# Four 32-column tiles in place of one 128-column matmul, in the MLP of an attention + MLP kernel

## The chip, the cores and the metric

The kernel runs on one core of a Trainium2 chip. Times are device microseconds (us) of one execution, medians over several executions. The record marks all timed runs used here as fast. Runs made once, for a look with a profile, have the state "unknown" and are compared only for effects of several microseconds, or by what their trace shows.

## The reference, cut to what matters

```python
scores = q @ k^T / 8 + decay, causal          # 64 (batch, head) pairs, 576 x 576, head 64
attn   = softmax(scores) @ v                  # gathered to x: 4608 tokens x 512
h      = x @ w_in                             # 512 -> 2048
out    = gelu_tanh(h) @ w_out                 # 2048 -> 512, float32
```

## The kernel before: the parts that matter

TensorE uses its array in three shapes, which the profile prints as rows*columns. Scores use 32 rows and 128 columns (32*128; each head's data lies on 32 partitions). Attention products use 128 rows and 32 columns (128*32). The MLP's matmuls used the full array (128*128), except where L368 stood beside attention products: there it was already cut into four tiles of 32 columns.

```python
    def mlp_in(c, prs):                       # hidden layer, 512 tokens at a time
        ...
                        nc.tensor.matmul(
                            ph[:, j, :],
                            w_in_sb[:, dt, 128 * ft:128 * ft + 128],
                            xT[:, dt, CH * c:CH * (c + 1)],
                            start=(dt == 0), stop=(dt == N_DT - 1))       # L330
    def mlp_in_half(half, g):                 # the first 512 tokens, 256 at a time
        ...
                    nc.tensor.matmul(
                        ph[:, j // 2, QA * (j % 2):QA * (j % 2) + QA],
                        w_in_sb[:, dt, 128 * ft:128 * ft + 128],
                        xT[:, dt, n0:n0 + QA], ...)                       # L347
    def mlp_out(c):
        ...
                    cols = 32 if by_columns else 128
                    for c0 in range(0, 128, cols):
                        nc.tensor.matmul(pso[c0:c0 + cols, m0:m1],
                                         gT[c % 2][:, ft, 128 * n + c0:128 * n + c0 + cols],
                                         w_out_sb[:, ft, m0:m1], ...)     # L368
```

L347 stands early in the kernel, while w_in, w_out, q, k and v are still being loaded. The keep-busy matmuls of zeros (L199) and the prefix sums stay full in both kernels.

The softmax here doesn't subtract the row's maximum and nothing guards it: scores larger than these inputs give would overflow.

Of the kernel before, what the change touches and what calls it, by code (L numbers as in the profile page):

```python
# [16 lines left out]
def kernel(  # L17
# [10 lines left out]
    nc = tc.nc  # L28
# [10 lines left out]
    N_DT = D_MODEL // 128  # L39
# [6 lines left out]
    CH = 512  # L46
# [12 lines left out]
    QA = 256  # L59
# [33 lines left out]
    def many(n, shape, dtype, name):  # L93
        return [singles.tile(shape, dtype, name=f"{name}{i}") for i in range(n)]
# [13 lines left out]
    xT = singles.tile([128, N_DT, B * S], BF16, name="xT")  # L108
    gT = many(2, [128, N_FT, CH], BF16, "gT")
    w_in_sb = singles.tile([128, N_DT, D_FF], BF16, name="w_in_sb")  # L110
# [91 lines left out]
    def scores(i, r, groups=((0, 1, 2, 3),)):  # L202

        qq, p = qT[i % 2], pt[i % 2]
        if i < 2:
            off, n = split_rounds[r]
            todo = [(key, col - off, q0, nq) for (key, col, q0, nq) in split_pieces[r]]
        else:
            off, n = rounds[r]
            todo = []  # L210
            for (key, col, q0, nq) in pieces:
                a, z = max(col, off), min(col + nq, off + n)
                if a < z:
                    todo.append((key, a - off, q0 + a - col, z - a))
        for heads in groups:
            tiles = {g: psS.tile([128, 2, 512], FP32, name="ps_s", tag="s") for g in sorted({h // 2 for h in heads})}
            for c in range(2):
                for j, (key, c0, q0, nq) in enumerate(todo):
                    for h in heads:
                        nc.tensor.matmul(  # L220
                            tiles[h // 2][:, h % 2, c0:c0 + nq],
                            key_columns(i, key, h, c),
                            qq[32 * h:32 * h + 32, q0:q0 + nq, c],
                            start=(c == 0 and j == 0), stop=(c == 1),
                            skip_group_check=True,
                        )
            for g, t in tiles.items():
                nc.scalar.activation(p[:, 2 * g:2 * g + 2, off:off + n], t[:, :, 0:n], AF.Exp, scale=scale)  # L228
# [93 lines left out]
    def mlp_in(c, prs):  # L322

        tiles = [psS.tile([128, 2, 512], FP32, name="ps_h", tag="s") for _ in prs]
        for pr, ph in zip(prs, tiles):
            for dts in (range(N_DT - 1), range(N_DT - 1, N_DT)):
                for j in range(2):
                    ft = 2 * pr + j
                    for dt in dts:
                        nc.tensor.matmul(  # L330
                            ph[:, j, :],
                            w_in_sb[:, dt, 128 * ft:128 * ft + 128],
                            xT[:, dt, CH * c:CH * (c + 1)],
                            start=(dt == 0), stop=(dt == N_DT - 1),
                        )
        for pr, ph in zip(prs, tiles):
            nc.scalar.activation(gT[c % 2][:, 2 * pr:2 * pr + 2, :], ph, AF.Gelu_apprx_tanh)  # L337

    def mlp_in_half(half, g):

        ph = psS.tile([128, 2, 512], FP32, name="ps_h", tag="s")
        n0 = QA * half
        for dts in (range(N_DT - 1), range(N_DT - 1, N_DT)):
            for j in range(4):
                ft = 4 * g + j
                for dt in dts:
                    nc.tensor.matmul(  # L347
                        ph[:, j // 2, QA * (j % 2):QA * (j % 2) + QA],
                        w_in_sb[:, dt, 128 * ft:128 * ft + 128],
                        xT[:, dt, n0:n0 + QA],  # L350
                        start=(dt == 0 and j % 2 == 0), stop=(dt == N_DT - 1),
                        skip_group_check=True,
                    )
        nc.scalar.activation(gT[0][:, 4 * g:4 * g + 4, n0:n0 + QA],
                             ph.rearrange("p a (b n) -> p (a b) n", n=QA), AF.Gelu_apprx_tanh)

    def mlp_out(c):

        for n in range(CH // 128):
            r0 = CH * c + 128 * n  # L360
            last = c == NCH - 1 and n == CH // 128 - 1
            st = ostage_pool.tile([128, D_MODEL], FP32, name="o_st", tag="o")
            for (m0, m1) in ((0, 384), (384, 512)) if last else ((0, D_MODEL),):
                pso = psM.tile([128, D_MODEL], FP32, name="pso", tag="m")
                for ft in range(N_FT):
                    cols = 32 if by_columns else 128
                    for c0 in range(0, 128, cols):
                        nc.tensor.matmul(pso[c0:c0 + cols, m0:m1],  # L368
                                         gT[c % 2][:, ft, 128 * n + c0:128 * n + c0 + cols],
                                         w_out_sb[:, ft, m0:m1],  # L370
                                         start=(ft == 0), stop=(ft == N_FT - 1), skip_group_check=True)
                    if ft == N_FT - 1:
                        nc.vector.tensor_copy(st[:, m0:m1], pso[:, m0:m1])  # L373
                        eng = nc.scalar if m0 else nc.sync
                        eng.dma_start(out=out[r0:r0 + 128, m0:m1], in_=st[:, m0:m1])
                    yield
# [56 lines left out]
                cum_ps[:rows, t0 * BH:t1 * BH].rearrange("p (t i h) -> p t i h", i=NQ, h=4),  # L433
                AF.Exp, scale=-1.0, bias=shift[:rows, :])

    by_columns = []

    def pull(it, n):
        for _ in range(n):
            if next(it, False) is False:  # L440
                return
# [1 line left out]
    fills = {}  # L443
    dmas = {}

    def out_part(c, n, tiled=0):
        by_columns[:] = [True] * tiled
        pull(fills.setdefault(c, mlp_out(c)), n)

    def cast_w(copy):  # L450
# [3 lines left out]
    def load_values(b, half):  # L454
# [29 lines left out]
        "WI": load_w_in,  # L484
        "WO": load_w_out,
        "I": lambda c, pr: mlp_in(c, (pr,)),
        "J": mlp_in_half,
        "F": out_part,
        "f": lambda c, n: out_part(c, n, 1),
        "B": keep_busy,  # L490
        "X": load_exp,
    }
# [12 lines left out]
    def beside(i, r, c, todo):  # L505

        if i is not None:
            scores(i, r)
        for n, x in enumerate(todo):
            if isinstance(x, int):  # L510
                out_part(c, x, 1)
            else:
                x()
            if n == 0 and i is not None:
                after_scores(i, r)

    def after_scores(i, r):
        mask(i, r)
        if r == 1:
            make_vw(i, nc.gpsimd)  # L520
        if r == 2:
            copy_low(i)

    def pair(i, j, c):

        D, V = (lambda q: lambda: denominators(q)), (lambda q, x, spare=False: lambda: attn_out(q, x, spare))
        beside(i, 0, c, [D(j), 12])
        beside(i, 1, c, [V(j, 0), 10])
        beside(i, 2, c, [V(j, 1), 9])
        if i + 1 < NQ:  # L530
            beside(i + 1, 0, c, [D(i), 10])
            beside(i + 1, 1, c, [V(i, 0), 5, V(i, 1), 4])
            scores(i + 1, 2)
            after_scores(i + 1, 2)
        else:
            beside(None, 0, c, [D(i), 10, V(i, 0), V(i, 1, True), 10])
# [11 lines left out]
    with tc.manual_schedule():  # L548
        setup()
        run(FRONT)  # L550
        for c in range(2, NCH):
            out_part(c - 1, CH)
            for pr in range(2):
                mlp_in(c, (pr,))
            if c + 1 < B:
                prepare(2 * c + 3, 2 * c + 4)
            if c + 2 < B:
                load_v(c + 2)
            for pr in range(2, NP):
                mlp_in(c, (pr,))  # L560
            if c + 1 < B:
                load_exp()
                out_part(c, 6)
                pair(2 * c + 3, 2 * c + 2, c)
        out_part(NCH - 1, CH)
# [30 lines left out]
```

## Time and profile before

| | before |
|---|---|
| median of 6 runs | 341.67 us (341.55 to 342.11) |
| span of the profiled run | 339.9 us |
| TensorE busy | 329.8 us (97%) |
| TensorE matmuls, and as many weight loads | 4241 |

The lines that show the bound and the pitches are in the prediction. Two more views follow. First the DMA queue that carries instructions: packets, megabytes, and the time that they took as a share of 16 DMA engines. A packet has 16 KB (0.54 MB in 33).

```profile
q8 instruction: 33, 0.54, 0.7%
```

Then the early stretch of L347 in TensorE's timeline (start, duration, group; "x96" counts instructions):

```profile
27.79 1.92 PE L347 MATMUL ps_h<-xT,w_in_sb 128*128 128x256 bf16 x16
29.64 1.22 PE L274 MATMUL po_m<-pt,vw 128*32 128x320 bf16 x40
30.79 10.65 PE L347 MATMUL ps_h<-xT,w_in_sb 128*128 128x256 bf16 x96
41.28 1.46 PE L368 MATMUL pso<-w_out_sb,gT 128*128 128x512 bf16 x6
```

96 matmuls start within 41.28 - 30.79 = 10.49 us, 109 ns each, with nothing between them. ("128x256" means 256 moving columns: the columns of the operand that streams through the array.)

### The profile page before, as it was taken

The numbers are of one execution on the slowest core, as the hardware profiler recorded it, in microseconds if no ns is written. First come the engines' busy times: TensorE is split into PE (matmuls) and PEld (weight loads), VectorE is DVE, ScalarE is ACT, GpSimd is POOL, SyncE is SP. The second block draws the span as 40 slices with busy tenths as digits, with TensorE's granted clock in tenths as the row PEclk, the third lists the DMA queues.
The fourth block names the chain that finished last, engine by engine and source line by source line (L and its number), as shares of the span: only waits on it lengthen the run. The fifth ranks groups of instructions, "written<-read, shape, count | busy, mean of one in ns | idle before, by whom it ended". The sixth has DMA issues, their size and how long they took to land.

```text
span 339.9 us, 9423 instructions
## 1 busy us (share of the span) xinstructions
PE 329.8 (97%) x4241; PEld 162.0 (48%) x4241; DVE 132.3 (39%) x206; ACT 191.8 (56%) x201; POOL 110.1 (32%) x155
## 2 busy tenths in 40 slices
PE   3999999999999999999999999999999999999996
PEld 1458844544454445444444444444544454444443
DVE  4686059830465435703462244413430450021011
ACT  4784686677547665667566665674576624502510
POOL 8987551600506233601551145106410410000000
PEclk9999999999999999999999999999999999999999
DMA  7999999570316970591129210910100010011012
GB/s 127 207 216 214 196 230 194 102 172 2 95 36 101 227 156 33 131 205 39 35 77 207 59 67 35 212 30 35 63 31 2 33 63 34 2 62 62 0 40 85
DMA packets 40201, 33.26 MB, mean 98 GB/s; under 512 B 27473, under 2 KB 29777, under 8 KB 40161
## 3 DMA queue, kind: packets, MB, share of 16 engines
q0 software_dynamic: 8848, 16.58, 27.4%
q1 hardware_dynamic: 31168, 16.01, 17.0%
q8 instruction: 33, 0.54, 0.7%
q10 hardware_dynamic: 144, 0.07, 0.1%
q14 instruction: 8, 0.06, 0.0%
HBM read 36.85 MB, written 9.44 MB: 136 GB/s over the span
## 4 chain that ended last, share of the span: by engine, by line
PE 90%; DMA 2%; POOL 2%; ACT 2%; DVE 1%; issue 1%; POOLq 0%; DVEq 0%; ACTq 0%
PE pso L368 36%; PE ps_h L330 33%; PE po L288 8%; PE ps_s L220 8%; PE ps_h L347 4%; DMA v_nat<-in_v_dram 2%; ACT pt L228 2%; PE po_m L274 1%; POOL vw L178 1%; POOL v_nat L132 0%; PE ps_o L288 0%; DVE pt L263 0%; DVE vw L178 0%; POOL pt L234 0%; POOL q_c L155 0%
## 5 line engine op out<-in xcount | busy, mean ns | idle before, releaser
L368 PE MATMUL pso<-w_out_sb,gT 128*32 128x512 bf16 (+3 forms) x1492 | 134.5, 377 | 0.0
L228 ACT ACTIVATE pt<-ps_s 128x1024 bf16<-128x1024 f32 (+2 forms) x100 | 93.7, 988 | 53.6 <-PE ps_s L220 46.0
L330 PE MATMUL ps_h<-xT,w_in_sb 128*128 128x512 bf16 x512 | 111.9, 379 | 0.0
L337 ACT ACTIVATE gT<-ps_h 128x1024 bf16<-128x1024 f32 x64 | 65.5, 1024 | 64.1 <-PE ps_h L330 64.1
L234 POOL TENSOR_SCALAR_AFFINE_SELECT pt<-pt 128x512 bf16<-128x512 bf16 (+3 forms) x65 | 38.2, 597 | 140.6 <-ACT pt L228 139.7
L368 PEld LDWEIGHTS <-gT 128*32 128x32 bf16 (+1 forms) x1492 | 56.3, 97 | 56.8 <-issue 3.5
L330 PEld LDWEIGHTS <-w_in_sb 128*128 128x128 bf16 x512 | 50.0, 98 | 60.4 <-issue 0.4
L373 DVE COPY o_st<-pso 128x512 f32<-128x512 f32 (+2 forms) x37 | 24.9, 673 | 71.8 <-PE pso L368 71.5
L307 DVE STREAM_TRANSPOSE den<-po 128x576 f32<-128x576 f32 x14 | 11.0, 784 | 65.7 <-PE po L288 65.7
L220 PE MATMUL ps_s<-qT,kT 32*128 32x64 bf16 (+5 forms) x896 | 36.2, 264 | 0.2 <-ACT pt L228 0.2
L319 DVE TENSOR_TENSOR xT<-po,rb 128x576 bf16<-128x576 f32 x26 | 19.7, 757 | 31.6 <-PE po L288 31.5
L178 POOL TENSOR_TENSOR vw<-v_nat,wT 128x1280 bf16<-128x1280 f32 (+1 forms) x13 | 30.0, 2308 | 0.1
L220 PEld LDWEIGHTS <-kT 32*128 32x128 bf16 x896 | 16.4, 93 | 23.7 <-issue 18.8
L161 DVE STREAM_TRANSPOSE kT<-k_c 128x576 f32<-128x576 f32 x16 | 20.0, 1248 | 16.9 <-DMA k_c<-in_k_dram 16.8
L288 PE MATMUL po<-pt,vw 128*32 128x64 bf16 (+4 forms) x624 | 22.4, 278 | 0.0
L161 DVE STREAM_TRANSPOSE qT<-q_c 128x576 f32<-128x576 f32 x16 | 19.9, 1244 | 1.2 <-PE ps_s L220 0.7
L288 PEld LDWEIGHTS <-vw 128*32 128x32 bf16 x672 | 14.2, 97 | 11.8 <-issue 3.7
L132 POOL DMA_DIRECT2D v_nat<-in_v_dram x20 | 15.3, 776 | 3.4 <-DMA w_out_sb<-in_moe_w_out_dram 3.4
L347 PE MATMUL ps_h<-xT,w_in_sb 128*128 128x256 bf16 x128 | 14.5, 273 | 0.0
L347 PEld LDWEIGHTS <-w_in_sb 128*128 128x128 bf16 x128 | 12.3, 98 | 1.7
L311 DVE STREAM_TRANSPOSE rb<-rec 128x576 f32<-128x576 f32 (+2 forms) x18 | 12.8, 711 | 0.6
L155 POOL DMA_DIRECT2D k_c<-in_k_dram x16 | 9.1, 568 | 11.3 <-DVE kT L161 5.7
(61 smaller groups left out, 124.9 us busy)
## 6 DMA issues: line engine op xcount, KB each, us to landing
out_dram<-o_st SPq DMA_DIRECT2D x35, 256.0 KB, 2.1
k_c<-in_k_dram POOLq DMA_DIRECT2D x16, 288.0 KB, 6.8
q_c<-in_q_dram POOLq DMA_DIRECT2D x16, 288.0 KB, 7.4
v_nat<-in_v_dram SPq DMA_DIRECT2D x16, 256.0 KB, 8.3
w_in_sb<-in_moe_w_in_dram POOLq DMA_DIRECT2D x4, 512.0 KB, 9.5
w_out_sb<-in_moe_w_out_dram POOLq DMA_DIRECT2D x4, 512.0 KB, 7.2
v_nat<-in_v_dram SPq DMA_DIRECT2D x16, 128.0 KB, 3.3
v_nat<-in_v_dram POOLq DMA_DIRECT2D x13, 128.0 KB, 7.9
```

Of the source, the lines that this page charges most:

```text
L161: nc.vector.transpose(out=dst.rearrange("p s c -> p (s c)").bitcast(FP32) .rearrange("p (t a) -> p a t", a=S // 32), in_=src.rearrange("p ...
L178: eng.tensor_mul(vw[i % 2][:, t0:t1], vb[:, t0:t1, h0:h0 + 4, :], wT[:, i, t0:t1, :].unsqueeze(3).to_broadcast([128, t1 - t0, 4, D]))
L220: nc.tensor.matmul(tiles[h // 2][:, h % 2, c0:c0 + nq], key_columns(i, key, h, c), qq[32 * h:32 * h + 32, q0:q0 + nq, c], start=(c == 0 an ...
L228: nc.scalar.activation(p[:, 2 * g:2 * g + 2, off:off + n], t[:, :, 0:n], AF.Exp, scale=scale)
L234: nc.gpsimd.affine_select(out=x, in_=x, compare_op=ALU.is_ge, fill=0.0, base=0, pattern=pattern, channel_multiplier=-1)
L288: nc.tensor.matmul(po[r0:r0 + w.shape[-1], 448 + q0:448 + q0 + nq], w, p[:, h, col:col + nq], start=(key in (0, "low")), stop=(key in ("lo ...
L319: nc.vector.tensor_mul(xT[:, 2 * u + x, S * b + s0:S * b + s1], po, rbs[i, part])
L330: nc.tensor.matmul(ph[:, j, :], w_in_sb[:, dt, 128 * ft:128 * ft + 128], xT[:, dt, CH * c:CH * (c + 1)], start=(dt == 0), stop=(dt == N_DT ...
L337: nc.scalar.activation(gT[c % 2][:, 2 * pr:2 * pr + 2, :], ph, AF.Gelu_apprx_tanh)
L347: nc.tensor.matmul(ph[:, j // 2, QA * (j % 2):QA * (j % 2) + QA], w_in_sb[:, dt, 128 * ft:128 * ft + 128], xT[:, dt, n0:n0 + QA], start=(d ...
L368: nc.tensor.matmul(pso[c0:c0 + cols, m0:m1], gT[c % 2][:, ft, 128 * n + c0:128 * n + c0 + cols], w_out_sb[:, ft, m0:m1], start=(ft == 0), ...
L373: nc.vector.tensor_copy(st[:, m0:m1], pso[:, m0:m1])
```

## The change

The intent: if all matmuls of the MLP use the column shape, as the attention products do, fewer changes of the array's shape are left. The core of the diff (the flag that chose the shape of L368 goes as well):

```diff
-                        nc.tensor.matmul(
-                            ph[:, j, :],
-                            w_in_sb[:, dt, 128 * ft:128 * ft + 128],
-                            xT[:, dt, CH * c:CH * (c + 1)],
-                            start=(dt == 0), stop=(dt == N_DT - 1),
-                        )
+                        for c0 in range(0, 128, 32):
+                            nc.tensor.matmul(
+                                ph[c0:c0 + 32, j, :],
+                                w_in_sb[:, dt, 128 * ft + c0:128 * ft + c0 + 32],
+                                xT[:, dt, CH * c:CH * (c + 1)],
+                                start=(dt == 0), stop=(dt == N_DT - 1),
+                                skip_group_check=True,
+                            )
 ... (L347 in the same way)
-                    cols = 32 if by_columns else 128
-                    for c0 in range(0, 128, cols):
+                    for c0 in range(0, 128, 32):
```

More of the change, by code (lines that the diff above doesn't have):

```diff
@@ L346, in mlp_in_half @@
                 for dt in dts:
-                    nc.tensor.matmul(
-                        ph[:, j // 2, QA * (j % 2):QA * (j % 2) + QA],
-                        w_in_sb[:, dt, 128 * ft:128 * ft + 128],
-                        xT[:, dt, n0:n0 + QA],
-                        start=(dt == 0 and j % 2 == 0), stop=(dt == N_DT - 1),
-                        skip_group_check=True,
-                    )
+                    for c0 in range(0, 128, 32):
+                        nc.tensor.matmul(
+                            ph[c0:c0 + 32, j // 2, QA * (j % 2):QA * (j % 2) + QA],
+                            w_in_sb[:, dt, 128 * ft + c0:128 * ft + c0 + 32],
+                            xT[:, dt, n0:n0 + QA],
+                            start=(dt == 0 and j % 2 == 0), stop=(dt == N_DT - 1),
+                            skip_group_check=True,
+                        )
         nc.scalar.activation(gT[0][:, 4 * g:4 * g + 4, n0:n0 + QA],
@@ L365, in mlp_out @@
                 for ft in range(N_FT):
-                    cols = 32 if by_columns else 128
-                    for c0 in range(0, 128, cols):
-                        nc.tensor.matmul(pso[c0:c0 + cols, m0:m1],
-                                         gT[c % 2][:, ft, 128 * n + c0:128 * n + c0 + cols],
+                    for c0 in range(0, 128, 32):
+                        nc.tensor.matmul(pso[c0:c0 + 32, m0:m1],
+                                         gT[c % 2][:, ft, 128 * n + c0:128 * n + c0 + 32],
                                          w_out_sb[:, ft, m0:m1],
@@ L434, in make_w @@
                 AF.Exp, scale=-1.0, bias=shift[:rows, :])
-    by_columns = []
     def pull(it, n):
@@ L444, with out_part @@
     dmas = {}
-    def out_part(c, n, tiled=0):
-        by_columns[:] = [True] * tiled
+    def out_part(c, n):
         pull(fills.setdefault(c, mlp_out(c)), n)
@@ L488 @@
         "F": out_part,
-        "f": lambda c, n: out_part(c, n, 1),
+        "f": out_part,
         "B": keep_busy,
@@ L510, in beside @@
             if isinstance(x, int):
-                out_part(c, x, 1)
+                out_part(c, x)
             else:
```

## The prediction

> **What bounds the kernel now.** I read the page first: busy time by engine, then the chain of work that ended last.
>
> ```profile
> span 339.9 us, 9423 instructions
> PE 329.8 (97%) x4241; PEld 162.0 (48%) x4241; DVE 132.3 (39%) x206; ACT 191.8 (56%) x201; POOL 110.1 (32%) x155
> ...
> PE 90%; DMA 2%; POOL 2%; ACT 2%; DVE 1%; issue 1%; POOLq 0%; DVEq 0%; ACTq 0%
> PE pso L368 36%; PE ps_h L330 33%; PE po L288 8%; PE ps_s L220 8%; PE ps_h L347 4%; DMA v_nat<-in_v_dram 2%; ACT pt L228 2%; PE po_m L274 1%; POOL vw L178 1%; POOL v_nat L132 0%; PE ps_o L288 0%; DVE pt L263 0%; DVE vw L178 0%; POOL pt L234 0%; POOL q_c L155 0%
> ```
>
> TensorE is the bound: 97% busy, and the three lines that the change touches (L330 and L347, which form the hidden layer, and L368, which forms the output) carry 33 + 4 + 36 = 73% of the chain. ACT, next, is busy 56%. So what matters is how fast TensorE streams these lines, not who waits for it. From about 23 us on the chain is almost nothing but TensorE.
>
> A busy share does not tell the rate, since pipelined matmuls overlap. So next I took the groups by shape. In "128*32" the first number is the rows of the array in use and the second the columns.
>
> ```profile
> L330 PE MATMUL ps_h<-xT,w_in_sb 128*128 128x512 bf16 x512 | 111.9, 379 | 0.0
> L368 PE MATMUL pso<-w_out_sb,gT 128*32 128x512 bf16 x1200 | 71.4, 379 | 0.0
> L368 PE MATMUL pso<-w_out_sb,gT 128*128 128x512 bf16 x260 | 59.7, 379 | 0.0
> ...
> L347 PE MATMUL ps_h<-xT,w_in_sb 128*128 128x256 bf16 x128 | 14.5, 273 | 0.0
> ```
>
> The kernel before already has the new form: 1200 tiles of 32 columns are 300 sets of four, beside 260 full matmuls of the same 512 columns. So the change is priced from this trace. The timeline of TensorE gives the pitch, from the start of one run to the start of the next:
>
> ```profile
> 205.98 1.25 PE L368 MATMUL pso<-w_out_sb,gT 128*32 128x512 bf16 x20
> 207.06 0.86 PE L288 MATMUL po<-pt,vw 128*32 128x512 bf16 x24
> 207.74 1.04 PE L368 MATMUL pso<-w_out_sb,gT 128*32 128x512 bf16 x16
> 208.71 0.63 PE L220 MATMUL ps_s<-qT,kT 32*128 32x320 bf16 x16
> 209.27 1.90 PE L368 MATMUL pso<-w_out_sb,gT 128*128 128x512 bf16 x8
> 211.01 13.98 PE L330 MATMUL ps_h<-xT,w_in_sb 128*128 128x512 bf16 x64
> 224.82 1.46 PE L368 MATMUL pso<-w_out_sb,gT 128*128 128x512 bf16 x6
> 226.21 0.69 PE L220 MATMUL ps_s<-qT,kT 32*128 32x64 bf16 x24
> ```
>
> Five sets of four tiles (x20) take 207.06 - 205.98 = 1.08 us, 0.216 us a set; what follows them is in columns too. Sixty-four full matmuls take 224.82 - 211.01 = 13.81 us, 0.2158 us each. **A set of four tiles and a full matmul cost the same.** Where the shape of the array changes, something is added: four sets before the scores take 0.97 us, 4 x 0.216 = 0.864 and 0.106 more; six full matmuls before the scores take 1.39 us, 1.296 and 0.094 more. A change of shape costs some 0.095 us.
>
> [...] 0.095 us at a change of shape, none between L368 in columns and L288 in columns. [...] a load of 128x32 took 97 ns in the mean and one of 128x128 took 98, and the four loads of a set overlap (29.3 us busy for 300 sets, 98 ns a set). [...] the median distance inside a set is 4 ns here. [...]
>
> **The change part by part.**
>
> *Streaming, L330 and the rest of L368.* 512 + 260 full matmuls of 512 columns, and 16 of 384, become sets of four. At 0.216 us against 0.216 us the difference is 0.
>
> *Changes of shape.* I walked through the order of TensorE's instructions and counted shape changes, three shapes besides the transposes at the start: rows (scores, 32*128), columns (attention products and tiles), full. Before there are 123. With L330, L347 and L368 all in columns there are 117: seven go and one comes. Most do not go, because a full run stands between two runs of scores: full-to-rows becomes columns-to-rows and costs the same. The seven that go lie where a full run touches a run in columns: five around the 256-column runs at 25.3 to 30.8 us, one at 56.4 us, one at 279.6 us. The one that comes is in front of the keep-busy matmuls of zeros at 42.6 us, which stay full. All lie on the chain, so 6 x 0.095 = **-0.57 us**.
>
> *Instructions.* 512 + 128 + 292 full matmuls gain three matmuls and three weight loads each: 932 x 6 = 5592 more on 8482. A set is 8 instructions. At 512 columns TensorE must be given one every 216 / 8 = 27 ns; at 384, 163 / 8 = 20 ns; at 256 (L347, pitch 109 ns from 10.49 us for 96), 13.7 ns; in the last 16 sets of 128 columns (pitch 56 ns), 7 ns. How fast instructions can come is shown by a busy stretch of before:
>
> ```profile
> 118.47:134.15 15.68, 15.68 (x382) 7.72 (x384) 6.78 (x11) 9.49 (x11) 6.31 (x8) 1.00 0.48 109
> 30.79:41.28 10.49, 10.49 (x104) 9.40 (x97) 2.83 (x4) 5.12 (x5) 7.07 (x9) 1.00 1.22 194
> ```
>
> In the first stretch 382 matmuls and 384 loads went in 15.68 us, 20.5 ns each, with TensorE never idle. [...] That covers the 512-column sets (27 ns) for good. It does not prove 13.7 ns over the 96 sets of the second stretch (768 instructions), nor 7 ns at the end. [...] In the tail 128 instructions take 0.9 us now[...]. The short stretches have passed 128 instructions at 15.4 ns each[...], so I lean to an issue rate well below 22 ns and put the expected cost at 0.6 us for L347 and 0.1 for the tail. This is a choice, not a reading.
>
> *Waits.* Each group still ends with one last matmul, so GELU and the eviction start when they did. Buffers are the same.
>
> Sum: 341.56 - 0.57 + 0.6 + 0.1 = 341.7 us.
>
> **The rivals.** (1) *Issue becomes the bound* also in the long 512-column runs: 64 sets, 512 instructions in a row, where before had at most 12 sets in a row. Every 1 ns above 27 costs 8 ns a set over some 770 sets, 6 us. Against it: 20.5 ns was kept over 766 instructions. At worst this ends slower by over 2%. (2) *Mode changes matter more than counted*, for instance if coming back to full weights costs loads that columns hide. Against it: after the scores, full and column runs begin alike (286 and 283 ns after a 448-column score). Even if all 39 changes between rows and full saved 0.1 us the gain would be 3.9 us, 1.1%. (3) *Loads become the bound*: a set needs 98 ns of overlapped loading and L347 has 109 ns. Against it: attention sets of 64 columns follow each other 28 ns apart in columns, so loads overlap further. (4) *Clock*: the granted clock was 1.00 in all stretches, in columns too; I expect no change.
>
> **Range and chances.** The best case is every instruction in time: 341.0 us, and 340.6 with noise. The upper end takes most of the 5.2 us: 345.5. Over 348.4 (+2%) needs rival 1; under 334.7 (-2%) needs a gain of 7 us, [...]. So faster 0.01, same 0.95, slower 0.04.
>
> **What would show it.** Right: a pitch of 0.216 us per set in L330, so 13.8 us for 64 sets; 117 changes of shape at 0.095 us; the granted clock at 1.00. The undecided step: the 96 sets of L347 take 10.5 us if issue keeps up, up to 15.7 if not; the starts inside a set would then spread from 4 ns to the issue interval. Wrong: L330 at over 0.22 us per set, TensorE idle with "issue" as the reason, or instruction fetches (0.5 MB before, which must grow to some 0.9 MB) that stall it.

The sum is 341.56 - 0.57 + 0.6 + 0.1 = 341.7 us (0.6 us for L347 and 0.1 us for the tail). The two short runs of 16 sets add no term, and the two terms are the author's choice. Without them the sum is 341.0 us, the best case. The 22 ns is the 20.5 ns of the busy stretch with an allowance added. The worst case of 5.2 us, which the range and the 15.7 us of L347 use, came out of the cut reckoning too; as an estimate from the trace alone it is the same: 768 instructions at 20.5 ns are 15.7 us, 5.2 us more than the 10.49 us measured. Beside the gain of 7 us: the cost of all 123 changes of shape, 123 x 0.095 = 11.7 us, of which 117 stay.

## The result, and the profile after

| | before | after |
|---|---|---|
| median of 6 runs | 341.67 us | 354.15 us (351.34 to 355.36) |
| span of the profiled run | 339.9 us | 352.5 us |
| TensorE matmuls | 4241 | 7037 |

The changed kernel is slower: the ratio of the runs is 1.0353, with a 95% interval of 1.0316 to 1.0389. Ratios here are the mean time of one kernel's fast runs over that of the other's of the same rounds, so they are not quite the ratios of the medians.

The page of the changed kernel, with the chain of work that ended last, the 256-column groups of the hidden layer (L350, which was L347), and the instruction queue:

```profile
PE 332.7 (94%) x7037; PEld 173.4 (49%) x7037; DVE 132.1 (37%) x206; ACT 191.7 (54%) x201; POOL 110.1 (31%) x155
...
q8 instruction: 55, 0.90, 1.0%
...
PE 91%; issue 4%; POOL 3%; ACT 1%; DVE 0%; POOLq 0%; ACTq 0%
...
L350 PE MATMUL ps_h<-xT,w_in_sb 128*32 128x256 bf16 x512 | 16.8, 290 | 9.3 <-issue 9.3
```

TensorE is still the chain, but its busy share fell from 97% to 94%, and "issue", time in which the engine waited for nothing that the profile shows, went from 1% to 4% of the chain. The group line says where: TensorE sat idle for 9.3 us before instructions of L350, and no semaphore ended that idle time. The timeline shows how:

```profile
27.43 0.52 PE L350 MATMUL ps_h<-xT,w_in_sb 128*32 128x256 bf16 x12
29.67 1.60 PE L350 MATMUL ps_h<-xT,w_in_sb 128*32 128x256 bf16 x52 [1.72 <-issue]
31.09 1.22 PE L274 MATMUL po_m<-pt,vw 128*32 128x320 bf16 x40
32.13 1.17 PE L350 MATMUL ps_h<-xT,w_in_sb 128*32 128x256 bf16 x36
35.59 3.68 PE L350 MATMUL ps_h<-xT,w_in_sb 128*32 128x256 bf16 x128 [2.30 <-issue]
42.34 3.68 PE L350 MATMUL ps_h<-xT,w_in_sb 128*32 128x256 bf16 x128 [3.07 <-issue]
48.26 4.25 PE L350 MATMUL ps_h<-xT,w_in_sb 128*32 128x256 bf16 x92 [2.24 <-issue]
52.33 1.48 PE L370 MATMUL pso<-w_out_sb,gT 128*32 128x512 bf16 x24
```

Four gaps of 1.7 to 3.1 us. Between gaps there are 128 matmuls (52 + 40 + 36, then 128, then 128), and as every matmul has its weight load, **256 instructions: exactly one page**. Inside a page the sets of four tiles run at the old pitch, 108 to 110 ns. In the trace, packets of the instruction queue start at 27.07, 33.25, 39.92 and 45.93 us and take about 1 us each, and TensorE goes on 1.4 to 1.6 us after each has ended. That reads as TensorE having run out of instructions and waiting for a page; the experiments test it.

There is a second cost. At the end of the fourth gap the granted clock of TensorE is halved for 3.4 us, from 48.08 to 51.50 us, and 16 sets go at some 213 ns instead of 109. The clock fell 2.06 us into the fourth gap, but the longest gap, 3.07 us, was followed by full clock. What makes it fall stays open here.

I then lined up the two traces matmul by matmul, with four tiles counted as one, and asked where the difference of start times grows. It is -0.02 us at 23 us, +11.08 us when L350 is done, unchanged to 102 us, +12.05 us at 126 us of the kernel before (two more gaps put down to issue, of 0.49 and 0.45 us between two tiles of a set), 0.12 us less at 279 us where a change of shape is gone, and 0.65 us are added at the very end. **Nearly all of the 12.6 us is in 27 us of the kernel, in L350.** The 11.1 us there are 9.98 us of gaps beyond the streaming time, some 1.65 us of half clock (16 sets at 104 ns more) and about -0.5 us of saved shape changes.

### The profile page after: what moved, and what is told of

Read it like the earlier page. It is cut to its first block, busy times and chain, and to the rows that moved or that the text cites. A ratio compares the mean times of both kernels' runs of the same rounds, so it can differ in the third digit from the quotient of the medians.

```text
span 352.5 us, 15015 instructions
## 1 busy us (share of the span) xinstructions
PE 332.7 (94%) x7037; PEld 173.4 (49%) x7037; DVE 132.1 (37%) x206; ACT 191.7 (54%) x201; POOL 110.1 (31%) x155
## 4 chain that ended last, share of the span: by engine, by line
PE 91%; issue 4%; POOL 3%; ACT 1%; DVE 0%; POOLq 0%; ACTq 0%
PE pso L370 35%; PE ps_h L331 32%; PE ps_s L220 9%; PE po L288 8%; PE ps_h L350 5%; PE po_m L274 1%; PE idle_ps L199 1%; ACT pt L228 1%; POOL v_nat L132 1%; POOL vw L178 1%; PE ps_o L288 0%; DVE pt L263 0%; POOL pt L234 0%; PE cum_ps L431 0%; POOL q_c L155 0%
## 5 line engine op out<-in xcount | busy, mean ns | idle before, releaser
L370 PE MATMUL pso<-w_out_sb,gT 128*32 128x512 bf16 (+2 forms) x2368 | 135.2, 374 | 0.1
L331 PE MATMUL ps_h<-xT,w_in_sb 128*32 128x512 bf16 x2048 | 112.4, 379 | 0.1
L339 ACT ACTIVATE gT<-ps_h 128x1024 bf16<-128x1024 f32 x64 | 65.5, 1023 | 64.7 <-PE ps_h L331 64.7
L370 PEld LDWEIGHTS <-gT 128*32 128x32 bf16 x2368 | 59.4, 97 | 54.2 <-issue 3.6
L331 PEld LDWEIGHTS <-w_in_sb 128*32 128x32 bf16 x2048 | 55.4, 97 | 55.6 <-issue 1.0
L350 PE MATMUL ps_h<-xT,w_in_sb 128*32 128x256 bf16 x512 | 16.8, 290 | 9.3 <-issue 9.3
L288 PEld LDWEIGHTS <-vw 128*32 128x32 bf16 x672 | 14.3, 97 | 11.6 <-issue 3.7
L350 PEld LDWEIGHTS <-w_in_sb 128*32 128x32 bf16 x512 | 14.8, 103 | 10.6 <-issue 10.1
L357 ACT ACTIVATE gT<-ps_h 128x1024 bf16<-128x1024 f32 x8 | 8.2, 1023 | 18.8 <-PE ps_h L350 18.8
```

Source lines behind the costliest of these rows:

```text
L288: nc.tensor.matmul(po[r0:r0 + w.shape[-1], 448 + q0:448 + q0 + nq], w, p[:, h, col:col + nq], start=(key in (0, "low")), stop=(key in ("lo ...
L331: nc.tensor.matmul(ph[c0:c0 + 32, j, :], w_in_sb[:, dt, 128 * ft + c0:128 * ft + c0 + 32], xT[:, dt, CH * c:CH * (c + 1)], start=(dt == 0) ...
L339: nc.scalar.activation(gT[c % 2][:, 2 * pr:2 * pr + 2, :], ph, AF.Gelu_apprx_tanh)
L350: nc.tensor.matmul(ph[c0:c0 + 32, j // 2, QA * (j % 2):QA * (j % 2) + QA], w_in_sb[:, dt, 128 * ft + c0:128 * ft + c0 + 32], xT[:, dt, n0: ...
L370: nc.tensor.matmul(pso[c0:c0 + 32, m0:m1], gT[c % 2][:, ft, 128 * n + c0:128 * n + c0 + 32], w_out_sb[:, ft, m0:m1], start=(ft == 0), stop ...
```

## The experiments

Theory 1: TensorE's instructions come in pages of 256; while loads keep the DMA busy a page takes about 6 us to come (5.92, 6.75 and 5.92 us between the restarts above); a stretch that uses up a page faster than that waits for the difference. L350 uses one in 3.5 us (32 sets at 109 ns). Rivals: the added instructions cost as such, wherever they stand; short column matmuls are slow in themselves; a page takes 6 us at any time (theory 1b). Theory 1 as against 1b, with loads as the cause, is called 1a in the later expectations.

### Only L347 in columns

```diff
 (kernel before)
+                    for c0 in range(0, 128, 32):   # in L347 alone
```

> The kernel before with only the 256-column matmuls of L347 as four tiles; the 512-column ones stay full. Theory 1 (instruction supply): TensorE's instructions come in pages of 256, a page needs about 6 us to come while the loads keep the DMA busy, and only a stretch that uses up 256 instructions in less time waits. Then nearly the whole loss is here: 352.5 us (351.5 to 354), with gaps of 2 to 3 us put down to issue, 256 instructions apart. Rival (the number of added instructions as such, spread over the kernel): L347 has 768 of the 5592 added, so some 2 us of loss, 343 to 344.

Measured: 351.91 us median (350.77 to 353.19, 4 runs), ratio 1.0298 (1.0268 to 1.0328). The trace has four gaps put down to issue, of 1.8, 3.4, 2.8 and 2.5 us from the start of one matmul to the next, all in L347 (now L348):

```profile
29.83 1.60 PE L348 MATMUL ps_h<-xT,w_in_sb 128*32 128x256 bf16 x52 [1.54 <-issue]
36.58 3.68 PE L348 MATMUL ps_h<-xT,w_in_sb 128*32 128x256 bf16 x128 [3.12 <-issue]
42.77 3.68 PE L348 MATMUL ps_h<-xT,w_in_sb 128*32 128x256 bf16 x128 [2.52 <-issue]
48.69 4.36 PE L348 MATMUL ps_h<-xT,w_in_sb 128*32 128x256 bf16 x92 [2.24 <-issue]
```

The rest of the kernel runs level with the kernel before. 768 of the 5592 added instructions carry 10.3 us (of the medians) of the 12.5 us lost. The rival "instructions as such" is out as the main cause.

### All but L347 in columns

```diff
 (changed kernel)
-                    for c0 in range(0, 128, 32):   # in L350 alone
```

> The changed kernel with only L347 back to full matmuls. Theory 1: 342.5 us (341.5 to 343.5), what is left being two stalls of some 0.5 us near 120 us and the end. Rival (added instructions as such): 4824 of 5592 are still there, so 351 to 353.

Measured: 343.71 us median (342.93 to 346.4, 4 runs), ratio 1.0079 (1.0033 to 1.0126). That is 0.2 us over the range that I gave, and one run of four is at 346.4 without a trace to say why. In the profiled run one gap is left (0.66 us at 122.7 us, between two tiles of a set), and the end is again 0.65 us later. So 4824 added instructions cost some 0.8% (0.3 to 1.3%).

### L347 as two tiles of 64 columns

```diff
 (changed kernel)
-                    for c0 in range(0, 128, 32):
+                    for c0 in range(0, 128, 64):   # in L350, with slices of 64
```

> The changed kernel with L347 as two tiles of 64 columns: half the instructions, 27 ns each, so 256 of them last 7.0 us. Theory 1: as a page needs some 6 us, next to no stall in L347: 341.5 to 344 us. Rival (a 256-column matmul in column tiles is slow in itself, by its loads or its shape): about half the loss stays, 347 us, and gaps are spread over all sets instead of 256 instructions apart.

Measured: 342.89 us median (342.25 to 346.7, 4 runs), ratio 1.0056 (1.0001 to 1.0112).

```profile
30.74 10.67 PE L350 MATMUL ps_h<-xT,w_in_sb 128*64 128x256 bf16 x192
41.34 1.48 PE L370 MATMUL pso<-w_out_sb,gT 128*32 128x512 bf16 x24
```

The 96 sets take 41.34 - 30.74 = 10.60 us without a gap. With a page lasting 7.0 us instead of 3.5, the loss in this stretch is gone, not halved: a threshold, as theory 1 has it, and not a cost per tile.

### A page measured by itself, with the DMA nearly idle

In the kernel before, the hidden layer of the last chunk is cut into 128 moving columns and four tiles. 256 sets of 8 instructions would take 14.3 us at 56 ns a set, 1.8 us a page: faster than pages come, so the gaps show the time of a page.

```diff
 (kernel before, last chunk only, L330)
+                        for m0 in range(0, CH, 128):
+                            for c0 in range(0, 128, 32):
+                                nc.tensor.matmul(ph[c0:c0 + 32, j, m0:m0 + 128], ...)
```

> The kernel before, with the hidden layer of the last chunk (64 x 512 columns, 13.8 us, DMA nearly idle) as 256 sets of four column tiles with 128 moving columns: 2048 instructions, 8 pages of 256, 56 ns a set if nothing holds it. It measures the time of a page where no load is under way. Theory 1a (a page takes about 6 us because loads hold the DMA): 2 to 4 us a page, so the stretch takes 16 to 32 us. Theory 1b (a page takes about 6 us always): 8 x 6.2 = 50 us, the kernel 378 us. Rival (the queue itself issues no faster than some ns each): no gaps, but an even pitch longer than 56 ns.

Measured: 355.71 us, one run. TensorE's timeline:

```profile
309.04 3.30 PE L340 MATMUL ps_h<-xT,w_in_sb 128*32 128x128 bf16 x221
314.22 1.97 PE L340 MATMUL ps_h<-xT,w_in_sb 128*32 128x128 bf16 x128 [1.88 <-issue]
317.94 1.97 PE L340 MATMUL ps_h<-xT,w_in_sb 128*32 128x128 bf16 x128 [1.76 <-issue]
321.67 1.97 PE L340 MATMUL ps_h<-xT,w_in_sb 128*32 128x128 bf16 x128 [1.76 <-issue]
```

After each page of 128 matmuls and 128 loads comes a gap; from restart to restart 3.72 or 3.73 us, and some 3.45 twice later. Inside a page a set of 8 instructions takes 56 ns, 7 ns an instruction. So how fast the queue issues is no limit here, and a page with the DMA nearly idle (share 0.04 from 309 to 340 us) takes 3.45 to 3.73 us. Theory 1b is out already; that loads make the difference is still to be shown.

### The form of L350, late, with and without loads

The same place with 256 moving columns, which is what L350 does early. First alone, then with six loads of 1 MB each (w_out again, into a buffer that is no longer read), released when the chunk before has its last GELU; then the loads alone beside full matmuls.

```diff
 (256 columns)                 +  for m0 in range(0, CH, 256): for c0 in range(0, 128, 32): ...
 (loads, after the last GELU of chunk 7)
+                for x in range(6):
+                    ins = nc.gpsimd.dma_start(out=pt[x // 3]..., in_=w_out_hbm[:, n * (x % 4):n * (x % 4 + 1), :])
+                    after(ins, done)
```

> The kernel before, with the hidden layer of the last chunk as 128 sets of four column tiles with 256 moving columns: the form of L347 in the changed kernel, 1024 instructions in 13.9 us, at a time when the DMA is nearly idle. The run with 128 columns measured 3.45 to 3.73 us a page of 256 instructions there; these pages last 3.5 us. Theory 1a (a page takes 6 us or more only while loads hold the DMA): gaps of 0 to 0.25 us a page, the kernel 341.5 to 343 us. Theory 1b (short column tiles stall as in L347 wherever they stand): 4 gaps of 2 to 3 us, 350 us or more.

> The same with six loads of 1 MB (w_out again, into a buffer that is no longer read) running beside the last chunk's hidden layer. Theory 1a: pages take 5 to 6.7 us, as in L347 of the changed kernel, and TensorE has gaps of 1.5 to 3 us each 256 instructions: 347 to 353 us. If the loads don't matter to the pages: as without them, 341.5 to 343 us.

> Control: the kernel before (full matmuls throughout) with the same six loads. Both theories: the loads alone cost nothing, 341 to 342.5 us, as 128 instructions in 13.8 us need half a page.

Measured: alone 341.83 us, with the loads 344.09, loads beside full matmuls 342.12 (the kernel before on the same chip: 341.65). Alone:

```profile
308.70 14.16 PE L340 MATMUL ps_h<-xT,w_in_sb 128*32 128x256 bf16 x512
322.79 14.03 PE L379 MATMUL pso<-w_out_sb,gT 128*128 128x512 bf16 x80
```

The very instructions that lose 11 us early lose nothing late: 128 sets in 322.79 - 308.70 = 14.09 us, one run without a gap. With six loads the range I had given was missed: there was only one long gap, of 1.58 us idle, and two of some 0.2. The loads ran until some 318 us (DMA share 1.15 from 317 to 318 us, 0.14 in the next). The packet of the first page with a gap fell among them; the next one started at 317.85 us, as they ended. That is how theory 1 would read it, but one gap could be chance. So the loads were made longer.

### Ten loads in place of six

```diff
-                for x in range(6):
+                for x in range(10):
```

> The late 256-column stretch with ten loads of 1 MB beside it, where six had ended after 316 us and only the first page fell among them (one gap of 1.7 us). Theory 1a: now all pages of the stretch fall among loads, so three or four gaps of 1.5 to 3 us, 6 us or more in sum: 347 to 353 us. If the one gap of the run with six loads was chance: 344 us or less again.

> Control: the kernel before, all full, with the same ten loads. Loads alone cost nothing or a little at the end: 341.5 to 343 us, no gap of TensorE in the last chunk.

> The measure of a page under load: the late stretch with 128 moving columns (a page lasts 1.8 us) and ten loads. Without loads a page took 3.45 to 3.73 us. Theory 1a: 5 to 6.7 us a page while the loads last, falling to 3.5 after them. Theory 1b: 3.5 to 3.7 us throughout.

Measured: 348.06 us with 256-column tiles, 341.98 us with full matmuls, one run each. The timeline of the first:

```profile
308.61 6.29 PE L340 MATMUL ps_h<-xT,w_in_sb 128*32 128x256 bf16 x221
316.08 3.68 PE L340 MATMUL ps_h<-xT,w_in_sb 128*32 128x256 bf16 x128 [1.18 <-issue]
322.00 3.68 PE L340 MATMUL ps_h<-xT,w_in_sb 128*32 128x256 bf16 x128 [2.24 <-issue]
327.93 1.16 PE L340 MATMUL ps_h<-xT,w_in_sb 128*32 128x256 bf16 x35 [2.25 <-issue]
```

The loss of the early stretch stands here at the end of the kernel, made by loads: three gaps, 5.92 and 5.93 us from restart to restart. The control had full matmuls and the same load. The stretch from 316 to 323 us in the two runs (engine busy times, clock, DMA share, GB/s), tiles first. The DMA share is the time of all packets summed over 16 engines, and packets overlap, so it can pass 1:

```profile
316.00:323.00 7.00, 4.67 (x165) 4.47 (x168) 0.00 (x0) 2.05 (x2) 0.00 (x0) 1.00 1.24 206
```

```profile
316.00:323.00 7.00, 7.00 (x34) 3.19 (x33) 0.00 (x0) 4.09 (x4) 0.00 (x0) 1.00 1.24 207
```

At the same DMA share of 1.24, TensorE is busy all 7.00 us with full matmuls, and 4.67 us with tiles. The loads do not slow matmuls; they slow pages. (Both traces lack single matmul records, which a list of gaps shows as 0.2 us with "issue"; they come at even distances in full stretches too.)

The third run, 128 columns with ten loads, took 362.62 us and measures the page under load:

```profile
315.66 3.60 PE L340 MATMUL ps_h<-xT,w_in_sb 128*32 128x128 bf16 x128 [3.56 <-issue]
321.58 3.41 PE L340 MATMUL ps_h<-xT,w_in_sb 128*32 128x128 bf16 x128 [2.32 <-issue]
327.78 3.39 PE L340 MATMUL ps_h<-xT,w_in_sb 128*32 128x128 bf16 x128 [2.79 <-issue]
331.51 1.97 PE L340 MATMUL ps_h<-xT,w_in_sb 128*32 128x128 bf16 x128 [0.34 <-issue]
```

5.92 and 6.20 us a page while the loads last, then 3.73 us, once 4.00, and 3.73 again. In this run the granted clock was halved in long stretches (0.50 from 316 to 323 us), so the matmuls of a page took 3.4 to 3.6 us in place of 1.97. That does not set the time of a page: the 256-column run with the same loads, at full clock, has 5.92 and 5.93 us. Without loads the next page's packet starts 1.1 us after TensorE's restart (314.22 to 315.34 us in the run without loads); with them 3.7 us after (315.66 to 319.33 us). The packet itself takes 0.9 to 1.4 us in both. In the 256-column run at full clock it starts 3.6 us after the restart, too (316.08 to 319.70 us, 322.00 to 325.65 us). So the extra time of 2.2 to 2.5 us a page passes before the packet starts. (The first such page without loads is 1.1 us to the packet's start, 1.35 us in the DMA and 1.25 us more until TensorE goes on; with loads it is 3.7, 1.0 and 1.3 us.) What the packet waits for no record shows, and that stays open.

### The changed kernel without the load of w_out

The same from the other side: take a load away where the stalls were. The output matmuls use w_in in its place, so the result is wrong; TensorE's instructions are the same.

```diff
 (changed kernel)
-                                         w_out_sb[:, ft, m0:m1],
+                                         w_in_sb[:, ft // 4, 512 * (ft % 4) + m0:512 * (ft % 4) + m1],
 ... (and the four loads of w_out taken out of the schedule, with the wait of one load of v for them)
```

> The changed kernel without the load of w_out (4 MB read), whose place w_in takes as an operand: wrong on purpose, same instructions on TensorE. The load of w_out falls into the 256-column stretch. Theory 1a: with less on the DMA there the pages come faster, so the gaps in L350 (10 us in sum) shrink by a half or more: 343 to 349 us. Theory 1b (pages take as long anyway): gaps as before, 352 to 355 us.

Measured: 348.17 us, one run. Two gaps are left in L350, of 1.54 and 2.75 us idle, 4.3 us in sum against 9.3. They stand where DMA is still busy (DMA share 1.05 and 1.06 in the two gaps themselves). From 33 to 40 us, the changed kernel and then this one:

```profile
33.00:40.00 7.00, 3.97 (x140) 3.58 (x132) 2.10 (x2) 2.05 (x2) 4.17 (x5) 1.00 1.08 166
```

```profile
33.00:40.00 7.00, 7.00 (x259) 6.83 (x249) 3.09 (x3) 3.98 (x4) 7.00 (x10) 1.00 0.65 111
```

With the DMA share down from 1.08 to 0.65, TensorE goes from 3.97 us busy to 7.00.

### An attempt at the rest

In three runs whose last block is in columns (the changed kernel, and the same with L347 full or in tiles of 64), the end comes 0.65 to 0.79 us later after the last matmul. In each of them a page of instructions is in the DMA just then, and the last big output's packets end 1.96 to 2.09 us after the last matmul instead of 1.25. In the run with only L347 in columns, whose last block is full, no page falls there, and they end at 1.25. So the last block was made full again, with L347 in tiles of 64:

```diff
 (changed kernel with L347 in tiles of 64)
+                    w = 128 if last else 32
```

> An attempt to keep the gain and drop the costs: the changed kernel with L347 as two tiles of 64 and the last block of 128 rows (16 sets of 384 and 16 of 128 columns) full, so that no instruction page is fetched beside the last output (its packets ended 0.7 to 0.8 us later in the runs with columns there). Expected: 0.7 us under the run with 64-column tiles, about level with the kernel before, 341.2 to 342.6 us. If the end had another cause: 342.5 us or more.

Measured: 342.91 us median (342.06 to 344.29, 4 runs), ratio 1.0044 (1.0002 to 1.0086). In the profiled run no page falls on the end and the packets end at 1.26 us, so the cause of the late end is supported. But the median is not lower than with 64-column tiles alone, and at 342.91 us it is 0.3 us above the range given, where I had expected it "if the end had another cause": two runs of four took 1.7 and 2.2 us more than the other two, without a trace. What holds those runs is open. No version here beats the kernel before.

## Why the prediction was wrong

**Streaming: right.** A set of four tiles streams like a full matmul: 216 ns at 512 columns, 163 at 384, 109 at 256 and 56 at 128, medians of the changed kernel.

**Changes of shape: right.** 117 are left of 123, at 0.085 to 0.1 us; the gain shows as -0.12 us at 279 us and about -0.5 us in the early stretch.

**Rival 1, issue as the bound of the long 512-column runs: did not come.** In six of the eight runs of L331 (which was L330) 64 sets took 13.81 us; in the other two 13.88 and 14.11.

**Issue in L347: here it failed.** The term "0.6 us for L347", with 5.2 us as the worst case, was priced as a rate: so many ns for an instruction. The instruction supply was the right suspect, but in the trace it did not come at a rate, it came in pages of 256 (55 packets for 14074 instructions). The term measured 9.98 us of gaps. Inside a page issue was no limit: 7 ns an instruction in the 128-column run, where the rate that I had started from was 20.5. And the worst case was taken from a stretch with another load on the DMA: the two lines that I set beside each other have 0.48 and 1.22 in the column of the DMA share, and I did not read that column. At 0.48 the 20.5 ns an instruction, 5.2 us a page, showed only that pages came that fast there. With the DMA share at 1.1 to 1.2 in the changed kernel a page took 5.9 to 6.8 us from restart to restart, 23 ns an instruction or more, and 13.7 were asked.

**The short runs: wrong.** I put down no loss for the two runs of 16 sets. The second short run held the first gap, 1.72 us, after 12 of its 64 tiles; the first had none. What counted was where a page ended, not how long the run was.

**The clock: wrong,** "I expect no change". It halved for 3.4 us after the gaps, some 1.65 us.

**The tail:** 0.1 us was set down for issue there. It lost nothing to issue (56 ns a set); the 0.65 us at the end, of the output's packets, had no term.

**What would show it** named instruction fetches growing to 0.9 MB that stall TensorE as a sign of a wrong prediction. The queue carried 0.90 MB, and they did.

The range ended at 345.5 us because its upper end was that worst case, and the chance of slower was 0.04 for the same reason.

## What to carry to other kernels

Count the instructions that an engine uses up per microsecond, and hold them against the time of a page of 256, in the stretch's own DMA load: here 3.45 to 3.73 us with a nearly idle DMA (share 0.04) and 5.9 to 6.8 us beside bulk loads (share 1.1 to 1.2). Tiles that streamed as fast as one matmul were free here only while a page lasted longer than that: 512 moving columns (6.9 us a page) were about safe (the run with L347 full lost some 0.8% in all), 256 (3.5 us) lost 9.3 us in gaps among loads and none with the DMA nearly idle. (The loads added or taken away here were all issued from GpSimd; others were not tested.) In this kernel a gap put down to "issue" that returned every 256 instructions, with a packet of the instruction queue ending 1.25 to 1.6 us before each restart, pointed to a page, not a wait of the program.
